# Pairwise minima on VectorE for every unit, one instruction for both heads' scaled negative maxima, the first step of the cubic on ScalarE

## The chip, the core and the metric

The kernel runs on one core of a Trainium2 chip. The metric is device time in microseconds of one execution. A core has TensorE (PE: matmuls, with their weight loads shown as PEld), VectorE (DVE), ScalarE (ACT), GpSimd (POOL) and SyncE (SP, which here only issues DMAs). Each works through its own instructions in the order they were written into its program, and waits for the others through semaphores.

## The reference

Three stages follow each other. The first is attention with a top-32 mask on 4 batches of 8 heads, 576 rows and 64 columns:

```
scores = scale * np.matmul(q, k.transpose(0, 1, 3, 2))
kth = np.partition(scores, -top_k, axis=-1)[..., -top_k:-top_k + 1]   # top_k = 32
scores = np.where(scores >= kth, scores, -1e9)
attn = exp(scores - max) / (sum + 1e-9);  out = attn @ v
```

Its output, read as 2304 tokens by 512, goes through two dense stages with 2048 inner columns:

```
h = x @ w_in
P = a[0] + a[1]*h + a[2]*h2 + a[3]*h3            # h2 = h*h, h3 = h2*h
Q = 1 + |b[0]|*|h| + |b[1]|*h2
x = (P / (Q + 1e-6)) @ w_out                     # first dense stage
h = x @ w2_in;  out = (h * cos(h)) @ w2_out      # second dense stage
```

## The kernel before, in words

**Units.** Attention is cut into 72 units. A unit is a block of 128 query rows and a pair of heads (j = 0, 1). `qk` makes the scores of both heads on TensorE, ScalarE copies them to SBUF (tile `sS`, one of 128x576 per head), `topk` finds the 32nd largest score of each row, ScalarE takes the exponential (tile `e`), and `av` transposes `e` and multiplies it by v.

**Top-32.** VectorE's MAX8 gives the 8 largest of a row and MATCH_REPLACE8 strikes them out; four rounds give 32. To shorten the first rounds the row is folded: its left and right halves give 288 pairwise maxima (`big`, the upper half of `e`) and 288 pairwise minima (`low`). Rounds one and two work on `big` alone; the third looks at both. The maxima are always taken on VectorE. The minima are taken on VectorE for units in `DMIN`, here the first 18, and on GpSimd for the other 54, with integer arithmetic on the bit patterns: left plus right, then minus the maximum, which is two GpSimd instructions of 128x288 per head. The exponential needs the row's maximum times -0.125 as its bias: one GpSimd instruction of 128x1 per head (`nb`), 144 in all.

**Dense stages.** Tokens go through in 9 blocks of 256 (index k), the inner columns in 8 groups (index g), so 72 groups per stage; one group's tiles are 128x512. In `in1` ScalarE copies h out of PSUM (`w`), makes |h| and |b1||h|+|b0|, and later the reciprocal of Q through Ln and Exp; GpSimd makes `q` and starts the cubic: `u = -a3*w - a2` and `u = u*w`. `mid1` and `end1` finish the cubic and the quotient with four VectorE instructions that each read two tensors (SCALAR_TENSOR_TENSOR), ScalarE rounds to the high part of `gg`, GpSimd subtracts to get the low part. In the last block (k = 8) GpSimd's share is done by VectorE. `in2` and `mul2` make h*cos(h) with two more GpSimd subtractions or multiplications and one for the low part; VectorE's share there is `n`, a one-input instruction.

**Order.** The program is written in numbered pieces, five to a unit; a table of times (`timed`) gives the piece in which each step of the dense stages is written. Weights are converted in the first 80 pieces (VectorE, ScalarE and GpSimd work on tiles `raw`, `cb`, `ch`). The order on each engine is then set by a scheduler that walks through this program with its own model of durations, so that a change in one instruction's engine moves the rows around it. Nearly all vector, scalar and GpSimd instructions are issued through the helper `Windowed`, which is why the trace gives them all one line, L81; rows are told apart by the names of their tiles. The functions that the change touches are `topk` (L311) and `in1` (L452).

Of the kernel before, what the change touches and what calls it, by code (L numbers as in the profile page):

```python
# [10 lines left out]
F32 = mybir.dt.float32  # L11
F32R = mybir.dt.float32r
I32 = mybir.dt.int32
U32 = mybir.dt.uint32
AF = mybir.ActivationFunctionType
ALU = mybir.AluOpType
# [7 lines left out]
P = 128  # L24
# [3 lines left out]
SCALE = 0.125  # L28
# [25 lines left out]
WA, PA = 12, 90  # L54
WG, PG = 10, 90
N1, NU, N2, NST, NGG = 2, 2, 3, 4, 3
DMIN = range(18)
PV, PV2, PV3, PV4 = 0, 0, 0, 0
SGN = (0, 1, 2, 3)
SUBV = (3,)  # L60
# [2 lines left out]
DV1, DV2 = 8, 7  # L63
# [1 line left out]
SQ, OBB, EB = 3, 1, 2  # L65
QRB, QHB = 1, 1
LQ = 1
UA = 0
S0, MD, O1P, I2, O2, SB = 46, 4, 1, 2, 3, 4


# [19 lines left out]
def body(tc, out, qt, kt, vt, ident_d, w1_d, w1o_d, a_d, b_d, w2_d, w2o_d):  # L91
    nc = tc.nc
    V, A, G = Windowed(tc, nc.vector, WIN, PM), Windowed(tc, nc.scalar, WA, PA), Windowed(tc, nc.gpsimd, WG, PG)
    PE, SP = nc.tensor, nc.sync

    with ExitStack() as ctx:
        def pool(name, bufs=1, **k):
            return ctx.enter_context(tc.tile_pool(name=name, bufs=bufs, **k))
# [5 lines left out]
        sml = pool("sml", 4)  # L104
# [105 lines left out]
        na0, na1, na2, na3 = (nega[:, i:i + 1] for i in range(4))  # L210
# [100 lines left out]
        def topk(i):  # L311
            n, pr = units[i]
            tiles = st.pop(i)
            e = att.tile([P, 2, S], F32, tag="e", bufs=EB, name=f"e{i}")
            et[i] = e
            kb, t = n // 2, n % 2
            if i % 8 == 0:
                sums[kb] = sml.tile([P, 2, H], F32, tag="sum", bufs=2, name=f"sum{kb}")
            sm = sums[kb][:, t]
            hd = [sml.tile([P, 32], F32, tag="hd", name=f"hd_{i}_{j}") for j in range(2)]  # L320
            nb = [sml.tile([P, 1], F32, tag="nb", name=f"nb_{i}_{j}") for j in range(2)]
            big, low = ([e[:, j, hf * HALF:(hf + 1) * HALF] for j in range(2)] for hf in range(2))
            both = [e[:, j] for j in range(2)]

            def top(j, x, r):
                V.max(out=hd[j][:, 8 * r:8 * r + 8], in_=x[j])

            def drop(j, x, r):
                V.match_replace(out=x[j], in_to_replace=hd[j][:, 8 * r:8 * r + 8], in_values=x[j], imm_value=NEG)

            for j, s in enumerate(tiles):
                l, r = s[:, :HALF], s[:, HALF:]
                V.tensor_tensor(big[j], l, r, op=ALU.max)
                if i in DMIN:
                    V.tensor_tensor(low[j], l, r, op=ALU.min)
                else:
                    lw = low[j].bitcast(I32)
                    G.tensor_tensor(lw, l.bitcast(I32), r.bitcast(I32), op=ALU.add)
                    G.tensor_tensor(lw, lw, big[j].bitcast(I32), op=ALU.subtract)
                top(j, big, 0)  # L340
                G.tensor_scalar(nb[j], hd[j][:, 0:1], -SCALE, 0.0, op0=ALU.mult, op1=ALU.add)
                yield
            for step in (((drop, big, 0), (top, big, 1)), ((drop, big, 1), (top, both, 2)), ((drop, both, 2),)):
                for f, *x in step:
                    for j in range(2):
                        f(j, *x)
                yield
            for j, s in enumerate(tiles):
                top(j, both, 3)
                A.activation(e[:, j], s, AF.Exp, bias=nb[j], scale=SCALE)  # L350
            yield
            for j, s in enumerate(tiles):
                row = sm[:, 2 * pr + j:2 * pr + j + 1]
                if i in PMASK:
                    G.tensor_scalar(s, s, hd[j][:, 31:32], 1.0, op0=ALU.is_ge, op1=ALU.mult)
                    G.tensor_mul(e[:, j], e[:, j], s)
                    A.activation(s, e[:, j], AF.Copy, accum_out=row)
                else:
                    V.scalar_tensor_tensor(e[:, j], s, hd[j][:, 31:32], e[:, j], op0=ALU.is_ge, op1=ALU.mult, accum_out=row)
                yield  # L360
# [76 lines left out]
        def mm_in(m, k, g):  # L437
            h = ps_h.tile([P, 2, BT], F32, tag="h", name=f"h{m}_{k}_{g}")
            xh, xl = xhl[k] if m == 0 else x2hl[k]
            lo = lot.pop((m, k, g)).rearrange("p f (c t) -> p f c t", t=P)  # L440
            for i in range(2):
                f = 2 * g + i
                for c in range(NCC):
                    wh = whi[m][:, c, f * P:(f + 1) * P]
                    PE.matmul(h[:, i, :], wh, xh[:, c, :], start=(c == 0), stop=False)  # L445
                    PE.matmul(h[:, i, :], wh, xl[:, c, :], start=False, stop=False)  # L446
                    PE.matmul(h[:, i, :], lo[:, i, c, :], xh[:, c, :], start=False, stop=(c == NCC - 1))  # L447
            return h
# [3 lines left out]
        def in1(k, g):  # L452
            h = mm_in(0, k, g).rearrange("p a t -> p (a t)")
            w, q, r, u = (mo.tile([P, BT * 2], F32, tag="m1" + t, bufs=NU if t == "u" else N1, name=f"{t}{k}_{g}") for t in "wqru")
            A.activation(w, h, AF.Copy)
            A.activation(r, w, AF.Abs)
            A.activation(q, r, AF.Identity, scale=b1, bias=b0)
            E1 = V if k >= DV1 else G
            E1.tensor_mul(q, q, r)
            A.activation(r, q, AF.Ln, bias=qc)  # L460
            A.activation(r, r, AF.Exp, scale=-1.0)
            if g < UA and k < DV1:
                A.activation(u, w, AF.Identity, scale=na3, bias=na2)
            else:
                E1.tensor_scalar(u, w, na3, na2, op0=ALU.mult, op1=ALU.add)
            E1.tensor_mul(u, u, w)
            g1[k, g] = (q, r, u, w)

# [114 lines left out]
        for g in range(NG):  # L583
            need[in1, 0, g] = 8 * (g // 2) + 4
            need[out1, 0, g] = 8 * (g // 2) + 6 + 2 * (g % 2)
            need[in2, 0, g] = n_w1 + 4 * (g // 2) + 4
# [3 lines left out]
        for k in range(NB):  # L590
            for g in range(NG):
                s1 = S0 + 40 * k + 5 * g
                s2 = s1 + 5 * LB
                timed += [(s1, in1, k, g), (s1 + MD, mid1, k, g), (s1 + 5 * L1 - E1P, end1, k, g), (s1 + 5 * L1 + O1P, out1, k, g)]
                timed += [(s2 + I2, in2, k, g), (s2 + 5 * L2 + O2, out2, k, g), (s2 + M2P[g % SINB], mul2, k, g)]
            timed.append((s1 + 5 * L1 + SB, sub1, k, 0))
# [3 lines left out]
        for e in flat:  # L600
            if e[0] in (in1, in2):
                loads.append((need.get(e, 0), load_lo, 0 if e[0] is in1 else 1, e[1], e[2]))
            elif e[0] is out1:
                loads.append((need.get(e, 0), load_w1ol, e[1], e[2]))
            elif e[0] is out2:
                loads.append((need.get(e, 0), load_w2o, e[1], e[2]))
# [36 lines left out]
        def attention():  # L643
# [5 lines left out]
            for i in range(nu + 1):  # L649
# [6 lines left out]
                for x, a in held:  # L656
                    store_k(x, *a)
                held = [(prep(*a), a) for a in preps.get(i, [])]
                t = topk(i) if i < nu else iter([None] * 9)
                for p in range(5):  # L660
                    if p == 0 and prev is not None:
# [81 lines left out]
```

## Time and profile before

| | us |
|---|---|
| median of 3 runs (lowest, highest) | 1524.38 (1523.16, 1527.18) |
| the profiled execution's own time | 1523.97 |
| its span, first to last instruction | 1522.1 |

Around the span lie 1.9 us. In the rows below, a busy time is the union of an engine's instructions, "x" is a count, and an arrow to the left in a wait names what ended it. For the argument the span is cut in three: 0 to 345 us, in which weights are converted and the first 17 units run; 345 to 1325 us, in which the other 55 units and most groups of both dense stages run side by side; and 1325 to 1522 us, in which only dense groups are left.

### The profile page before, as it was taken

The page shows a single profiled execution, that of the slowest core. Times are in us where ns is not written, and L with a number is a line of the kernel's source. Part 1 is how long each engine was busy: PE and PEld are TensorE (multiplying, and loading weights), DVE is VectorE, ACT ScalarE, POOL GpSimd, SP SyncE. Part 2 cuts the span into 40 slices and gives each one's busy share as a digit, 9 for nine tenths or more (in the row PEclk, how much of TensorE's full clock was granted, in tenths as well). Part 3 has the DMA queues.
Part 4 walks back from the last instruction along what each step waited for, and adds up shares of the span by engine and source line. Part 5 has one row for each costly group of instructions (what it writes and reads, how often), then busy time and mean ns, then how long its engine had stood idle before and what let it go on. Part 6 is the DMA issues. An engine that isn't in the chain of part 4 may idle for free.

```text
span 1522.1 us, 25487 instructions
## 1 busy us (share of the span) xinstructions
PE 1292.7 (85%) x9016; PEld 1136.6 (75%) x9016; DVE 1350.9 (89%) x2537; ACT 985.9 (65%) x1657; POOL 1069.1 (70%) x982
## 2 busy tenths in 40 slices
PE   5676776667896889898998988998899899999988
PEld 2343664557895779788888877887889788889986
DVE  7999988999989998999999999989999999756633
ACT  6676776655665667676767666675677666666632
POOL 4778676875987788788879787888788788641000
PEclk9766788658998999999999999999999999999999
DMA  7885766764366646455775655555456677666777
GB/s 230 288 258 193 231 212 202 267 216 153 123 195 190 194 168 225 164 190 170 238 238 167 217 187 181 174 205 178 158 193 227 215 229 243 218 214 217 244 235 231
DMA packets 141552, 315.01 MB, mean 207 GB/s; under 512 B 12016, under 2 KB 28528, under 8 KB 141424
## 3 DMA queue, kind: packets, MB, share of 16 engines
q1 hardware_dynamic: 122832, 261.99, 52.3%
q10 hardware_dynamic: 18592, 51.39, 10.4%
q8 instruction: 71, 1.16, 0.3%
q14 instruction: 57, 0.47, 0.1%
HBM read 278.20 MB, written 35.13 MB: 206 GB/s over the span
## 4 chain that ended last, share of the span: by engine, by line
DVE 48%; PE 16%; POOL 14%; issue 8%; ACT 7%; DMA 6%; SPq 0%; ACTq 0%; POOLq 0%; DVEq 0%
DVE e L81 20%; DVE hd L81 11%; DVE u L81 9%; PE o L560 4%; DVE cb L81 3%; POOL u L81 3%; DVE q L81 3%; POOL e L81 3%; PE h L445 3%; PE h L447 3%; PE h L446 2%; POOL gg L81 2%; POOL q L81 2%; POOL cb L81 2%; DVE n L81 1%
## 5 line engine op out<-in xcount | busy, mean ns | idle before, releaser
L81 DVE MAX8 hd<-e 128x8 f32<-128x288 f32 (+1 forms) x576 | 330.7, 597 | 2.6
L81 DVE MATCH_REPLACE8 e<-hd,e 128x288 f32<-128x288 f32 (+1 forms) x432 | 231.8, 539 | 0.0
L560 PE MATMUL o<-w2o,gg 128*128 128x512 f32 x864 | 226.7, 401 | 5.2 <-DMA w2o<-w2o 4.8
L445 PE MATMUL h<-xh,w1hi 128*128 128x256 f32 x576 | 173.5, 301 | 20.3 <-ACT hs L81 13.3
L81 DVE SCALAR_TENSOR_TENSOR e<-sS,hd,e 128x576 f32<-128x576 f32 x144 | 173.6, 1209 | 13.0 <-ACT e L81 12.6
L560 PEld LDWEIGHTS o<-w2o,gg 128*128 128x128 f32 x864 | 157.3, 193 | 35.4 <-DMA w2o<-w2o 6.2
L502 PE MATMUL y<-gg,w1o 128*128 128x256 f32 x576 | 170.9, 297 | 10.3 <-ACT gg L81 10.1
L503 PE MATMUL y<-gg,w1o 128*128 128x256 f32 x576 | 171.2, 297 | 8.9 <-POOL gg L81 8.9
L446 PE MATMUL h<-xl,w1hi 128*128 128x256 f32 x576 | 169.2, 294 | 6.7 <-DVE xl L81 6.7
L445 PE MATMUL h<-x2h,w2hi 128*128 128x256 f32 x576 | 167.8, 291 | 7.5 <-ACT w L81 6.8
L447 PE MATMUL h<-x2h,lo 128*128 128x256 f32 x576 | 167.0, 290 | 3.4 <-DMA lo<-w2lo 3.4
L504 PE MATMUL y<-gg,w1ol 128*128 128x256 f32 x576 | 169.6, 294 | 0.2 <-DMA w1ol<-w1ol 0.2
L447 PE MATMUL h<-xh,lo 128*128 128x256 f32 x576 | 168.6, 293 | 0.0
L81 DVE TENSOR_TENSOR e<-sS 128x288 f32<-128x288 f32 x180 | 158.7, 907 | 8.5 <-ACT sS L81 4.5
L446 PE MATMUL h<-x2l,w2hi 128*128 128x256 f32 x576 | 165.8, 288 | 0.0
L81 ACT ACTIVATE e<-sS,nb 128x576 f32<-128x576 f32 x144 | 110.9, 774 | 79.8 <-DVE hd L81 76.3
L445 PEld LDWEIGHTS h<-xh,w1hi 128*128 128x128 f32 x576 | 115.1, 200 | 28.9 <-ACT hs L81 16.5
L81 ACT ACTIVATE sS<-sx 128x576 f32<-128x576 f32 x144 | 92.6, 643 | 61.6 <-DVE e L81 48.8
L81 POOL TENSOR_TENSOR e<-sS 128x288 int32<-128x288 int32 x108 | 116.1, 1083 | 20.8 <-PE pp16t L382 8.3
L502 PEld LDWEIGHTS y<-gg,w1o 128*128 128x128 f32 x576 | 115.2, 200 | 16.3 <-ACT gg L81 13.1
L503 PEld LDWEIGHTS y<-gg,w1o 128*128 128x128 f32 x576 | 114.6, 199 | 14.7 <-POOL gg L81 12.3
L81 POOL TENSOR_TENSOR cb<-cb,raw 128x512 int32<-128x512 int32 x64 | 92.8, 1451 | 44.4 <-DVE cb L81 39.6
(1170 smaller groups left out, 4122.3 us busy)
## 6 DMA issues: line engine op xcount, KB each, us to landing
w2o<-w2o SPq DMA_DIRECT2D x144, 512.0 KB, 4.4
lo<-w1lo SPq DMA_DIRECT2D x72, 512.0 KB, 3.9
w1ol<-w1ol SPq DMA_DIRECT2D x72, 512.0 KB, 4.0
lo<-w2lo SPq DMA_DIRECT2D x72, 512.0 KB, 4.4
k<-kdr ACTq DMA_DIRECT2D x44, 576.0 KB, 5.0
raw<-w SPq DMA_DIRECT2D x32, 512.0 KB, 4.8
v<-vt ACTq DMA_DIRECT2D x48, 320.0 KB, 3.7
qr<-qt ACTq DMA_DIRECT2D x36, 256.0 KB, 4.0
```

What stands on the lines that cost most here:

```text
L81: r = f(*a, **k)
L445: PE.matmul(h[:, i, :], wh, xh[:, c, :], start=(c == 0), stop=False)
L446: PE.matmul(h[:, i, :], wh, xl[:, c, :], start=False, stop=False)
L447: PE.matmul(h[:, i, :], lo[:, i, c, :], xh[:, c, :], start=False, stop=(c == NCC - 1))
L502: PE.matmul(y[:, c, :], w1o[:, f, cs], gh[:, i, :], start=(f == 0 and c % 2 == 0), stop=False, skip_group_check=True)
L503: PE.matmul(y[:, c, :], w1o[:, f, cs], gl[:, i, :], start=False, stop=False, skip_group_check=True)
L504: PE.matmul(y[:, c, :], wl[:, i, cs], gh[:, i, :], start=False, stop=(f == NF - 1), skip_group_check=True)
L560: PE.matmul(o[:, t, :], l[:, i, ts], wt[i][:, r], start=(f == 0 and r == 0 and l is gh), stop=(f == NF - 1 and l is gl), skip_group_check= ...
```

## The change

In `topk` the minima are one VectorE instruction per head for every unit; the two GpSimd instructions are gone, as is `DMIN`. The 8 largest of both heads go into one tile, and one VectorE instruction, written behind the first MAX8 of the second head, makes both heads' scaled negative maxima. In `in1` the first step of the cubic is an ACTIVATE on ScalarE in all 72 groups, where it was GpSimd's in 64 and VectorE's in 8.

```diff
-DMIN = range(18)
-UA = 0
@@ topk
-            hd = [sml.tile([P, 32], F32, tag="hd", name=f"hd_{i}_{j}") for j in range(2)]
-            nb = [sml.tile([P, 1], F32, tag="nb", name=f"nb_{i}_{j}") for j in range(2)]
+            hds = sml.tile([P, 2, 32], F32, tag="hd", bufs=2, name=f"hd_{i}")
+            hd = [hds[:, j] for j in range(2)]
+            nb = sml.tile([P, 2], F32, tag="nb", bufs=2, name=f"nb_{i}")
...
                 V.tensor_tensor(big[j], l, r, op=ALU.max)
-                if i in DMIN:
-                    V.tensor_tensor(low[j], l, r, op=ALU.min)
-                else:
-                    lw = low[j].bitcast(I32)
-                    G.tensor_tensor(lw, l.bitcast(I32), r.bitcast(I32), op=ALU.add)
-                    G.tensor_tensor(lw, lw, big[j].bitcast(I32), op=ALU.subtract)
+                V.tensor_tensor(low[j], l, r, op=ALU.min)
                 top(j, big, 0)
-                G.tensor_scalar(nb[j], hd[j][:, 0:1], -SCALE, 0.0, op0=ALU.mult, op1=ALU.add)
+                if j == 1:
+                    V.tensor_scalar_mul(nb, hds[:, :, 0], -SCALE)
...
-                A.activation(e[:, j], s, AF.Exp, bias=nb[j], scale=SCALE)
+                A.activation(e[:, j], s, AF.Exp, bias=nb[:, j:j + 1], scale=SCALE)
@@ in1
-            if g < UA and k < DV1:
-                A.activation(u, w, AF.Identity, scale=na3, bias=na2)
-            else:
-                E1.tensor_scalar(u, w, na3, na2, op0=ALU.mult, op1=ALU.add)
+            A.activation(u, w, AF.Identity, scale=na3, bias=na2)
```

The order on VectorE around the start of unit 44, before. A name's first number is the unit (for `e`, `sS`, `hd`, `nb`), the block (for `n3`, `u4`) and so on; MAX is MAX8. The second and third rows are the pairwise maxima of its two heads; the masked product of unit 43 is mixed in.

```order
L81 TENSOR_SCALAR n3_0_8252<-rr3_0_8249 128x512
L81 TENSOR_TENSOR e44_8289<-sS44_0_8078 128x288
L81 TENSOR_TENSOR e44_8289<-sS44_1_8084 128x288
L81 SCALAR_TENSOR_TENSOR e43_8087,sum5_7440<-sS43_1_7866,hd_43_1_8089,e43_8087 128x576
L81 MAX hd_44_0_8290<-e44_8289 128x8
L81 MAX hd_44_1_8291<-e44_8289 128x8
```

And the same place after the change:

```order
L79 TENSOR_TENSOR e44_8105<-sS44_0_7899 128x288 x2
L79 TENSOR_TENSOR e44_8105<-sS44_1_7905 128x288 x2
L79 MAX hd_44_8106<-e44_8105 128x8 x2
L79 MATCH_REPLACE e44_8105<-hd_44_8106,e44_8105 128x288
L79 SCALAR_TENSOR_TENSOR e43_7908,sum5_7276<-sS43_1_7692,hd_43_7909,e43_7908 128x576
L79 TENSOR_SCALAR nb_44_8107<-hd_44_8106 128x2
```

Each maximum now has its minimum directly behind it, four two-input instructions in a row, and the instruction for `nb` stands behind one strike-out and the masked product of the unit before.

GpSimd at the same place, before, from the start of unit 44's minima:

```order
L81 TENSOR_TENSOR e44_8289<-sS44_0_8078 128x288
L81 TENSOR_TENSOR e44_8289<-sS44_1_8084 128x288
L81 TENSOR_TENSOR rr3_0_8249<-rr3_0_8249,n3_0_8252 128x512
L81 TENSOR_TENSOR e44_8289<-e44_8289 128x288
L81 TENSOR_TENSOR gg1_4_2_8427<-u4_2_8170,gg1_4_2_8427 128x512
L81 TENSOR_TENSOR e44_8289<-e44_8289 128x288
L81 TENSOR_SCALAR nb_44_0_8292<-hd_44_0_8290 128x1
L81 TENSOR_SCALAR u4_3_8385<-w4_3_8382,nega_108 128x512
L81 TENSOR_SCALAR nb_44_1_8293<-hd_44_1_8291 128x1
L81 TENSOR_TENSOR q4_3_8383<-q4_3_8383,r4_3_8384 128x512
```

And after, from the same subtraction of `n3`:

```order
L79 TENSOR_TENSOR rr3_0_8065<-rr3_0_8065,n3_0_8068 128x512
L79 TENSOR_TENSOR u4_3_8196<-u4_3_8196,w4_3_8193 128x512
L79 TENSOR_TENSOR gg1_4_2_8238<-u4_2_7986,gg1_4_2_8238 128x512
L79 TENSOR_TENSOR q4_3_8194<-q4_3_8194,r4_3_8195 128x512
L79 TENSOR_TENSOR gg2_7_8248<-rr2_6_7657,gg2_7_8248 128x512
```

Only two-input instructions of 128x512 are left there; the seven shorter ones (four of 128x288, the two `nb`, the first step of `u`) are gone.

## Rows read from the trace of the kernel before

**Rows 1.** The page: span, busy times of the engines, shares of the last chain.
```profile
span 1522.1 us, 25487 instructions
...
PE 1292.7 (85%) x9016; PEld 1136.6 (75%) x9016; DVE 1350.9 (89%) x2537; ACT 985.9 (65%) x1657; POOL 1069.1 (70%) x982
...
DVE 48%; PE 16%; POOL 14%; issue 8%; ACT 7%; DMA 6%; SPq 0%; ACTq 0%; POOLq 0%; DVEq 0%
```

**Rows 2.** Three stretches: length, each engine's busy us (count), clock, DMA.
```profile
0.00:345.00 345.00, 235.83 (x1052) 166.29 (x1052) 322.82 (x593) 235.29 (x426) 242.78 (x228) 0.74 0.72 233
345.00:1325.00 980.00, 873.05 (x6673) 801.56 (x6674) 923.97 (x1777) 651.25 (x1089) 799.13 (x735) 0.96 0.59 193
1325.00:1522.00 197.00, 183.79 (x1292) 168.79 (x1290) 104.16 (x169) 99.41 (x143) 27.16 (x20) 0.98 0.69 228
```

**Rows 3.** Order of time: start us, duration us, engine, line, operation, tiles.
```profile
906.24 1.29 POOL L81 TENSOR_TENSOR gg<-rr,gg 128x512 fp32r<-128x512 f32 x1
...
906.38 1.71 DVE L81 SCALAR_TENSOR_TENSOR u<-u,nega,w 128x512 f32<-128x512 f32 x1
...
907.50 1.74 POOL L81 TENSOR_TENSOR q<-q,r 128x512 f32<-128x512 f32 x1
```

**Rows 4.** By tile, whole span: durations as least/median/most in ns, first and last start.
```profile
L81 DVE TENSOR_TENSOR e<-sS x180: 433/894/1912, 9.1 to 1308.5; 128x288 f32<-128x288 f32 x180
...
L81 DVE SCALAR_TENSOR_TENSOR u<-u,nega,w x72: 726/1128/1914, 180.5 to 1430.3; 128x512 f32<-128x512 f32 x72
...
L81 DVE TENSOR_SCALAR n<-rr x72: 376/427/1561, 383.7 to 1504.1; 128x512 f32<-128x512 f32 x72
...
L81 DVE TENSOR_SCALAR rs<-sum x18: 148/210/818, 80.0 to 1327.8; 128x8 f32<-128x8 f32 x18
...
L81 POOL TENSOR_TENSOR q<-q,r x64: 1259/1297/1862, 180.4 to 1336.9; 128x512 f32<-128x512 f32 x64
```

**Rows 5.** VectorE's groups, 345 to 1325 us: count, busy us, mean ns, idle before.
```profile
L81 DVE TENSOR_TENSOR e<-sS 128x288 f32<-128x288 f32 x112 | 99.5, 907 | 4.4 <-PE pp16t L382 1.1 <-PE pp64t L382 1.1 <-PE pp52t L382 0.6
...
L81 DVE TENSOR_SCALAR n<-rr 128x512 f32<-128x512 f32 x52 | 37.4, 719 | 4.1 <-ACT rr L81 4.1
...
L81 DVE TENSOR_SCALAR rs<-sum 128x8 f32<-128x8 f32 x13 | 4.1, 316 | 0.1
```

**Rows 6.** GpSimd's groups, 345 to 1325 us, same columns.
```profile
L81 POOL TENSOR_TENSOR e<-sS 128x288 int32<-128x288 int32 x108 | 116.1, 1083 | 20.8 <-PE pp16t L382 8.3 <-PE pp51t L382 3.6 <-PE pp39t L382 2.8
L81 POOL TENSOR_TENSOR e<-e 128x288 int32<-128x288 int32 x108 | 105.9, 986 | 11.0 <-DVE e L81 8.7 <-DVE rs L81 2.0
L81 POOL TENSOR_TENSOR gg<-u,gg 128x512 fp32r<-128x512 f32 x55 | 77.5, 1409 | 18.0 <-ACT gg L81 17.5
...
L81 POOL TENSOR_SCALAR u<-w,nega 128x512 f32<-128x512 f32 x55 | 51.1, 928 | 36.3 <-ACT w L81 36.2
L81 POOL TENSOR_SCALAR nb<-hd 128x1 f32<-128x1 f32 x110 | 41.0, 377 | 9.0 <-DVE hd L81 8.7 <-DVE rs L81 0.2
...
L81 POOL TENSOR_TENSOR kraw<-kraw 128x576 f32<-128x576 f32 x8 | 13.7, 1708 | 8.3 <-ACT kraw L81 8.2
```

**Rows 7.** VectorE's waits, 345 to 1325 us: total us, times, longest.
```profile
DVE e L81 <- POOL e L81: 18.9, 12, 3.8
DVE e L81 <- ACT e L81: 12.6, 15, 2.0
DVE u L81 <- POOL u L81: 7.5, 9, 1.2
```

**Rows 8.** ScalarE's group nearest to the new instruction, 345 to 1325 us.
```profile
L81 ACT ACTIVATE rr<-hs,quarter 128x512 f32<-128x512 f32 x52 | 37.5, 721 | 0.8
```

**Rows 9.** ScalarE's longest wait, 345 to 1325 us.
```profile
ACT gg L81 <- DVE u L81: 90.1, 40, 5.7
```

**Rows 10.** A stretch in which VectorE is hardly ever idle, columns as in rows 2.
```profile
100.00:150.00 50.00, 34.18 (x133) 19.97 (x132) 49.90 (x93) 34.86 (x65) 42.29 (x38) 0.67 0.66 211
```

## The prediction, made before the changed kernel ran

> **What bounds the kernel now.** I read the page first. VectorE is the busiest engine, 1350.9 of 1522.1 us, and it holds 48% of the chain that ended last; GpSimd holds 14% and ScalarE 7% [rows 1]. A mean over the span hides stages, so I cut it in three [rows 2]. From 345 to 1325 us VectorE is busy 924 of 980 us (94%), TensorE 873, GpSimd 799 (82%), ScalarE 651 (66%). From 1325 us on TensorE is busy 184 of 197 and VectorE 104: that tail belongs to TensorE, and what VectorE or ScalarE gain or lose in it costs nothing. So the middle stretch decides, and in it VectorE: its time there is its work plus 56 us of idleness.
>
> Its work, however, is not all work. The timeline shows why [rows 3]: GpSimd starts a two-input instruction at 906.24 that takes 1.29 us; VectorE starts a two-input one at 906.38 that takes 1.71 us, where the shortest of its kind takes 0.726 [rows 4]. It ends at 908.09, 0.56 us after GpSimd's has ended. GpSimd's next starts at 907.50 and takes 1.74, where 1.259 is the least. Each stands still while the other is in the middle of an instruction, and the profile books the standstill as busy time. VectorE's minima and maxima show the same spread: 0.433 at the least, 0.907 on average [rows 4, 5].
>
> I size this standstill for the middle stretch as count times (mean less least duration), over the seven large groups that show it: the pairwise maxima with 112 x (0.907 - 0.433) = 53 us are the first, `n` with 52 x (0.719 - 0.376) = 18 us the last [rows 4, 5]; the seven hold 495 instructions and come to 207 us, 0.42 us each. This is 21% of the stretch and larger than all idleness. The change acts on it from both sides: it takes instructions off GpSimd, and gives VectorE more that can be stopped.
>
> **What leaves GpSimd.** In the middle stretch the 216 integer instructions (116.1 + 105.9 us), 55 first steps of the cubic (51.1) and 110 `nb` (41.0): 314 of its 799 us, 39% [rows 6]. How much standstill goes with them? If a VectorE instruction that comes upon a running GpSimd instruction waits for its end, the mean wait goes with the sum of count times mean duration squared, since long ones are both met more often and waited for longer. Over GpSimd's twelve groups (734 instructions, from the sums on `e` with 108 x 1.083 squared = 127 to `kraw` with 8 x 1.708 squared = 23 [rows 6]) this sum is 1012; the four groups that go hold 127 + 105 + 47 + 16 = 295, or 29%. What stays are the long ones, 1.4 us each like `gg`. So 71% of the wait per VectorE instruction remains: 0.30 us instead of 0.42.
>
> The Trainium skill states the mechanism: "SBUF — State Buffer", section "SBUF: two separate sides", says that VectorE with two SBUF inputs and GpSimd compete for one shared pair of ports, and that whoever starts first holds it for its whole instruction. Rows 3 agree. Were the ports shared by bandwidth instead, the wait would fall with GpSimd's busy time, to 61%, and the sum below would come to about -9 us instead of +17.
>
> **What each edit costs on VectorE**, in the middle stretch if not said otherwise.
> - *Old instructions wait less:* 207 us x 0.29 = -60 us. Between nothing given back (0) and the share of busy time (-81) I take this, since rows 3 show a wait for the end of an instruction.
> - *110 more minima:* they are the same instruction as the maxima, at least 0.433 and at the measured mean 0.907 [rows 4, 5], so +48 to +100 us. I take 0.433 + 0.30 = 0.73: +80.
> - *72 `nb` on VectorE:* the trace has no 128x2 instruction; the nearest is `rs`, 128x8, 0.148 at the least and 0.316 on average [rows 4, 5], so +11 to +23 us. Its spread says that it is stopped too, so 55 at 0.148 + 0.71 x 0.168 = 0.27 are +15, and the 17 of the first stretch at 0.316 are +5; VectorE is full there, 49.9 of 50 us from 100 to 150 [rows 10], so they add to the end.
> - *Waits for GpSimd:* VectorE waited 18.9 us for the minima, and these waits cannot come back, since it now makes them itself: -19. It waited 7.5 us for `u` [rows 7]; with one GpSimd step fewer and a shorter queue I take half: -4. Both ends: 0 to -56, all idleness.
> - *First step of the cubic on ScalarE:* 72 instructions, and the nearest is the same operation on the same shape, 0.721 us [rows 8]; 55 x 0.721 = 40 us raise ScalarE from 66% to 71% of the middle stretch. I count nothing: ScalarE itself waits 90 us for VectorE's `u` [rows 9], and the step sits three VectorE steps ahead of that wait. If this cover is gone, up to 40 us show. The eight first steps that VectorE loses lie in TensorE's tail: nothing.
> - *New waits:* head 0's exponential now waits for head 1's first MAX8. The order puts `nb` 5 VectorE rows ahead of the masked product that needs the exponential in unit 43, and 19 in unit 44, 2 us or more against an exponential that ScalarE makes as soon as it is free; nothing.
>
> Sum: -60 + 80 + 15 + 5 - 23 = +17 us on the profiled execution's 1523.97, so 1541; that execution lies 0.4 us under the median, which changes nothing here.
>
> **Rivals.**
> 1. *Forecast: VectorE's added work outweighs what it gets back*, 1541 us. With one term at an end and the others as taken: minima at 0.907 gives 1561, at 0.433 gives 1508; waits not falling at all 1601, falling to 61% with the minima's wait 1515. Its own range is 1529 to 1575.
> 2. *VectorE runs without gaps: faster.* GpSimd goes from 82% to about 50% of the stretch, every chain through it shortens, and VectorE's idleness falls to what rows 10 show, 0.1 in 50 us or 2 in 980. Then 54 us of idleness go and not 23: 1541 - 31 = 1510. It decides if more than 40 of the 56 us go (17 beyond the 23). For it: GpSimd's waits lie in the chain with 14%. Against: the second largest wait, 12.6 us, is for ScalarE's exponential [rows 7], and ScalarE gets more work. With standstill by busy share it would be 1484. I put it at 1508.
> 3. *It cancels*, 1524: the terms are both near 80 us, and half a step in either closes them.
> 4. *Nothing is given back.* GpSimd's remaining instructions are all long, and they may come just when VectorE's chains of `q` and `u` run, since they feed them. Then each of the 110 minima costs 0.433 + 0.42 = 0.85, 94 us, `nb` 22, and the stalls give 23: 1524 + 93 = 1617. Against: rows 6 show that the integer instructions hold 222 us of GpSimd's time, and VectorE cannot wait for what isn't there.
>
> The Trainium skill's "Perfetto Trace Analysis", section "Optimizing Scalar/DVE Operations", speaks against the change: with VectorE saturated, moving work off it may pay, and this moves work onto it. Taken alone that is the undisturbed cost, 110 x 0.433 + 72 x 0.148 = 58 us, 1582 us; the same section adds that between VectorE and GpSimd it might not help, as they share a port.
>
> **How the numbers follow.** Forecast 0.50, gapless VectorE 0.30, cancelling 0.14, nothing given back 0.06. About 0.3% (4.6 us) is what a measurement of this kernel can tell from no change. Faster 0.30, same 0.14, slower 0.50 + 0.06 = 0.56. The range leaves out a tenth on each side: 1503, a little under the gapless case and the minima at their least, to 1575, the forecast with about half of the wait relief missing.
>
> **What would show it.** In the profile after: 288 pairwise instructions on VectorE with a mean near 0.73; its masked products and `u` steps shorter by about 0.12 us on average; `nb` near 0.27; no wait of VectorE for GpSimd's `e`; GpSimd about 485 us busy in the middle stretch; VectorE busier in total than 1351 by some 40 us. I am wrong if the pairwise instructions fall towards 0.45 (the standstill was the integer instructions' almost alone), or if VectorE's idleness in the middle drops to a few us; then it is faster. I am wrong the other way if VectorE starts to wait for ScalarE's `u` or exponential by tens of us.

## The result, and the profile after

The changed kernel takes 1543.78 us (median of 4 runs, 1542.35 to 1547.41), the kernel before 1525.18 (1523.16 to 1527.18). The ratio is 1.0126, with a 95% interval of 1.0103 to 1.0149: slower by 1.3%. The forecast was 1541. The profiled execution took 1547.41 us, 3.6 more than the median, so its trace shows a little more than the typical loss.

The page after, in the columns of [rows 1]:

```profile
span 1545.6 us, 25235 instructions
...
PE 1287.3 (83%) x9016; PEld 1139.7 (74%) x9016; DVE 1372.0 (89%) x2709; ACT 1031.3 (67%) x1729; POOL 755.2 (49%) x558
...
DVE 45%; PE 22%; ACT 7%; DMA 5%; issue 4%; POOL 2%; ACTq 0%; SPq 0%; DVEq 0%; POOLq 0%
```

GpSimd has lost 314 of 1069 us, and its share of the last chain fell from 14% to 2%. VectorE has only 21 us more, where the prediction looked for some 40. The three stretches after, cut where the last unit ends, to be set beside [rows 2]:

```profile
0.00:345.00 345.00, 220.12 (x1034) 156.64 (x1035) 319.69 (x600) 238.86 (x431) 218.37 (x184) 0.77 0.72 229
345.00:1345.00 1000.00, 881.69 (x6697) 813.09 (x6695) 953.92 (x1950) 688.75 (x1148) 514.35 (x358) 0.95 0.58 192
1345.00:1546.00 201.00, 185.44 (x1287) 170.00 (x1287) 98.43 (x161) 103.69 (x151) 22.47 (x17) 0.97 0.67 219
```

The middle has grown from 980 to 1000 us; VectorE is busy 954 us in it where it was 924, and idle 46 where it was 56. The tail is 4 us longer. VectorE's groups in the middle after (columns as in [rows 5]):

```profile
L79 DVE TENSOR_TENSOR e<-sS 128x288 f32<-128x288 f32 x220 | 186.1, 889 | 23.4 <-PE pp20t L377 5.2 <-PE pp60t L377 3.4 <-PE pp68t L377 2.9
...
L79 DVE SCALAR_TENSOR_TENSOR e<-sS,hd,e 128x576 f32<-128x576 f32 x110 | 118.9, 1085 | 12.6 <-ACT e L79 12.4
...
L79 DVE SCALAR_TENSOR_TENSOR u<-u,nega,r 128x512 f32<-128x512 f32 x56 | 50.6, 904 | 0.0
...
L79 DVE TENSOR_SCALAR n<-rr 128x512 f32<-128x512 f32 x52 | 21.4, 411 | 0.0
L79 DVE TENSOR_SCALAR nb<-hd 128x2 f32<-128x2 f32 x55 | 15.8, 288 | 0.0
```

And of the kernel before, two groups of the same view that did not stand in [rows 5]:

```profile
L81 DVE SCALAR_TENSOR_TENSOR e<-sS,hd,e 128x576 f32<-128x576 f32 x111 | 136.2, 1233 | 13.0 <-ACT e L81 12.6
...
L81 DVE SCALAR_TENSOR_TENSOR u<-u,nega,r 128x512 f32<-128x512 f32 x55 | 59.0, 1073 | 0.0
```

The reader is to see three things. The older two-input instructions are shorter, 1.233 to 1.085 and 1.073 to 0.904. `n` hardly stands still any longer: 0.719 to 0.411, where 0.376 was the least [rows 4, 5]. The mean of the pairwise instructions (the maxima and minima) has hardly moved, 0.907 to 0.889, and now there are twice as many of them. This mean hides two moves against each other, as the median shows when the row by tile is set beside the one in [rows 4], 894 against 459 ns:

```profile
L79 DVE TENSOR_TENSOR e<-sS x288: 399/459/1682, 8.8 to 1334.1; 128x288 f32<-128x288 f32 x144
```

Counted in the trace from 345 us on, 73 of 112 (65%) took more than 0.55 us before, 1.15 us on average; after, it is 104 of 220 (47%), with 1.38 us. The others took 0.45 us in both. So a smaller part of them is stopped, and those that are stopped stand longer. VectorE's waits in the middle after, to be set beside [rows 7]:

```profile
DVE e L79 <- ACT e L79: 12.4, 11, 2.6
DVE e L79 <- PE pp20t L377: 5.2, 1, 5.2
DVE u L79 <- POOL u L79: 4.1, 7, 1.1
```

The 18.9 us for GpSimd's `e` are gone and `u` has halved, as forecast. New are waits of the pairs for TensorE's transposes of the unit two back, whose tile `e` they overwrite: the row on `pp20t` is the longest of thirteen, 22 us in all, where before there were five with 4 us. In the tail, VectorE now waits for the step that went to ScalarE:

```profile
DVE u L79 <- ACT u L79: 24.4, 8, 5.2
```

These are the eight groups of the last block. Such a wait of tens of us was one of the prediction's signs that it is wrong; here the tail is 4 us longer, so most of it is hidden.

### The profile page after: what moved, and what is told of

It reads as the page before. It is cut to its first block, busy times and chain, and to the rows that moved or that the text cites. A ratio compares the mean times of both kernels' runs of the same rounds, so it can differ in the third digit from the quotient of the medians.

```text
span 1545.6 us, 25235 instructions
## 1 busy us (share of the span) xinstructions
PE 1287.3 (83%) x9016; PEld 1139.7 (74%) x9016; DVE 1372.0 (89%) x2709; ACT 1031.3 (67%) x1729; POOL 755.2 (49%) x558
## 4 chain that ended last, share of the span: by engine, by line
DVE 45%; PE 22%; ACT 7%; DMA 5%; issue 4%; POOL 2%; ACTq 0%; SPq 0%; DVEq 0%; POOLq 0%
DVE e L79 22%; DVE hd L79 9%; DVE u L79 8%; PE o L552 4%; PE h L440 3%; PE h L442 3%; PE h L441 3%; DVE q L79 2%; DMA lo<-w2lo 2%; ACT L79 1%; PE y L496 1%; PE y L495 1%; PE y L494 1%; DVE cb L79 1%; DMA w2o<-w2o 1%
## 5 line engine op out<-in xcount | busy, mean ns | idle before, releaser
L79 DVE TENSOR_TENSOR e<-sS 128x288 f32<-128x288 f32 x288 | 242.8, 885 | 29.1 <-PE pp20t L377 5.2
L79 POOL TENSOR_TENSOR rr<-rr,n 128x512 f32<-128x512 f32 x56 | 82.0, 1464 | 251.3 <-DVE n L79 236.4
L440 PE MATMUL h<-xh,w1hi 128*128 128x256 f32 x576 | 178.2, 309 | 19.4 <-ACT hs L79 9.8
L441 PE MATMUL h<-xl,w1hi 128*128 128x256 f32 x576 | 173.5, 301 | 3.5 <-DVE xl L79 3.5
L79 DVE SCALAR_TENSOR_TENSOR e<-sS,hd,e 128x576 f32<-128x576 f32 x144 | 157.1, 1095 | 19.9 <-ACT e L79 19.7
L442 PE MATMUL h<-xh,lo 128*128 128x256 f32 x576 | 171.7, 298 | 0.0
L79 POOL TENSOR_TENSOR u<-u,w 128x512 f32<-128x512 f32 x64 | 93.2, 1456 | 131.8 <-ACT u L79 131.6
L440 PEld LDWEIGHTS h<-xh,w1hi 128*128 128x128 f32 x576 | 120.0, 208 | 26.8 <-ACT hs L79 12.2
L494 PEld LDWEIGHTS y<-gg,w1o 128*128 128x128 f32 x576 | 116.5, 202 | 28.0 <-ACT gg L79 25.4
L495 PEld LDWEIGHTS y<-gg,w1o 128*128 128x128 f32 x576 | 116.4, 202 | 16.6 <-POOL gg L79 14.5
```

The lines of the kernel that those rows point to most:

```text
L79: r = f(*a, **k)
L494: PE.matmul(y[:, c, :], w1o[:, f, cs], gh[:, i, :], start=(f == 0 and c % 2 == 0), stop=False, skip_group_check=True)
L495: PE.matmul(y[:, c, :], w1o[:, f, cs], gl[:, i, :], start=False, stop=False, skip_group_check=True)
```

## The experiments

Each ratio is against runs of the kernel before on the same chip, whose medians were 1526.2, 1526.1 and 1528.2 us for the three sets of four.

| kernel | us | ratio (95%) |
|---|---|---|
| minima alone | 1505.7 | 0.987 (0.985 to 0.990) |
| `nb` alone | 1543.8 | 1.012 (1.010 to 1.014) |
| `u` alone | 1535.0 | 1.006 (1.004 to 1.008) |
| `nb` and `u` | 1533.5 | 1.004 (1.002 to 1.006) |
| minima and `nb` | 1549.1 | 1.015 (1.013 to 1.017) |
| minima and `u` | 1518.1 | 0.995 (0.993 to 0.997) |
| all three, other order | 1553.6 | 1.018 (1.017 to 1.020) |
| minima and `nb`, plus a GpSimd copy of `nb` | 1525.7 | 0.999 (0.998 to 1.001) |
| minima, `nb` on ScalarE | 1528.9 | 1.003 (1.001 to 1.004) |
| minima, one `nb` for both heads on GpSimd | 1525.1 | 0.999 (0.998 to 1.001) |
| minima, both heads in one instruction | 1486.0 | 0.973 (0.970 to 0.975) |
| all three, both heads in one instruction | 1481.5 | 0.972 (0.969 to 0.974) |

**Each part alone.** First the minima:

```diff
-DMIN = range(18)
+DMIN = range(72)
```

> The kernel before with one edit: all minima on VectorE. Standstill theory (VectorE is the bound; each of its two-input instructions pays 0.43 us plus a standstill that GpSimd's remaining instructions cause; old instructions wait less): 110 more minima at about 0.87 us are +90, the six other old groups give back about -45, the waits for GpSimd's minima -19, new waits for the transposes of e +10: slower by 20 to 35 us, so most of the loss of the whole change or more. Rival (what is taken off GpSimd comes back in full): 222 of GpSimd's us go, VectorE's standstill falls by 23% of 207 us and its idleness by 19 to 40: no change or faster, 1500 to 1525.

It is faster by 1.3%, 1505.7 us: the rival was right in direction and in size, and the theory of the prediction, by which the minima make the loss, does not hold for the minima alone. Its middle stretch:

```profile
345.00:1305.00 960.00, 857.19 (x6649) 787.23 (x6650) 915.63 (x1885) 647.25 (x1085) 602.19 (x517) 0.97 0.58 197
```

VectorE does 108 more minima there and is busy 916 us, 8 less than before; idleness falls from 56 to 44. The second part, `nb`, is the hunks on `hds` and `nb` in `topk`:

> The kernel before with one edit: the scaled negative maxima of both heads in one VectorE instruction, 72 of them, 144 GpSimd instructions of 128x1 gone. Standstill theory: 72 x 0.30 = +22 us on VectorE, almost nothing given back as the GpSimd instructions were short (2% of 207 us): slower by 10 to 22 us. Rival (GpSimd's order matters: it stood 47 us in wait for VectorE's maxima before nb): these waits go from GpSimd's queue and VectorE's waits for GpSimd shrink: within 5 us of before, or faster.

1543.8 us, slower by 1.2%: as much as the whole change loses, from one VectorE instruction per unit. The loss is what the theory said, 18 us, but the profile gives `nb` 34 us there, 0.476 each; GpSimd is busy 1039.6 us in that kernel, almost as long as before. The third, ScalarE's first step of the cubic:

> The kernel before with one edit: the first step of the cubic on ScalarE in all groups. Standstill theory: GpSimd loses 64 us, 5% of VectorE's standstill (-10 us) and half of its waits for u (-4), ScalarE's 52 us more are hidden: faster by 5 to 15 us. Rival (ScalarE has no room left: the 66% of its time hide a chain through Ln, Exp and the exponential): slower by 10 to 40 us, with VectorE's wait for ScalarE grown by that.

1535.0 us, slower by 0.6%. The theory missed, and the loss is under the range of the rival too. VectorE's waits for ScalarE's `u`, 24.6 us, all lie in the tail; counted from the end of the last masked product it is 196 us long and was 194 before, so they are hardly the loss. Then the changed kernel with the minima left on GpSimd:

> The changed kernel with the minima of units 18 to 71 left on GpSimd in integer arithmetic. Standstill theory: the sum of the two small parts, -10 and +16: 1515 to 1540, so that the minima are what makes the changed kernel slow. Rival (the minima are harmless and the loss is in nb or u): as slow as the changed kernel, 1540 to 1550.

1533.5 us lies in the theory's range, but beside the first result its conclusion is wrong: on top of `nb` and `u` the minima cost 10 us, alone they gain 20. So the parts do not add: -1.3, +1.2 and +0.6% would be +0.5, and the change is +1.3.

**Pairs of parts, and order alone.** Which part undoes the gain of the minima?

> The kernel before with two of the three edits: all minima and the scaled negative maxima on VectorE; the first step of the cubic stays on GpSimd. If the parts add, -20 (minima alone) + 18 (negative maxima alone) = 1524. If what the minima gain is lost as soon as the negative maxima leave GpSimd (GpSimd then stands at n and runs the rest in one go against the pairs, whose standstill rises from 0.39 to 0.50 us), it is as slow as the changed kernel without ScalarE's step, 1533 to 1545.

1549.1 us: `nb` costs 18 us alone and 43 on top of the minima. This is near the second expectation, 4 us above its range; the pairs' standstill rose to 0.46, not to 0.50.

> The kernel before with two of the three edits: all minima on VectorE and the first step of the cubic on ScalarE; the scaled negative maxima stay on GpSimd. If the parts add, -20 + 9 = 1515. If ScalarE's step is what spoils the gain of the minima (GpSimd's u waits for ScalarE, 130 us in the changed kernel), 1530 or more, and the pairs' standstill is near 0.50.

1518.1 us, near the sum of 1515: ScalarE's step is not what spoils the minima. How much another order by itself can do was tried with one number:

```diff
-S0, MD, O1P, I2, O2, SB = 46, 4, 1, 2, 3, 4
+S0, MD, O1P, I2, O2, SB = 46, 3, 1, 2, 3, 4
```

> The changed kernel with one number of the table of times altered: the first VectorE step of the cubic is written one piece earlier in all groups (MD 3 for 4). No instruction is added or taken away, so that this shows what another order alone does. If order is a minor thing, within 5 us of the changed kernel's 1544; if the parts' interaction of 10 to 30 us comes from where the scheduler puts rows, 10 us or more to either side, with the pairs' standstill moved with it.

1553.6 against 1543.8 us: +10, or 0.6%, with no instruction more or less; the pairs' mean is 0.868 against 0.885, so their standstill did not rise with it. Differences of about this size between the kernels, such as the +9 of `u` alone, are therefore not put down to a cause here. And it is one sample, not a bound: each of the other edits makes the scheduler reorder about as much. Of VectorE's instructions 1587 of 2637 (matched by kind and count) still have the same one behind them in this kernel as in the changed one; for the kernels without and with the copy, below, it is 1510 of 2645.

**Why `nb` costs more than its length.** Two thirds of the 43 us are VectorE's own `nb`, which is stopped as well. In the kernel with minima and `nb` it is busy

```profile
L81 DVE TENSOR_SCALAR nb<-hd 128x2 f32<-128x2 f32 x72 | 29.4, 409 | 0.1
```

and the pairs' group is 19 us longer than with the minima alone (the rows stand below). The question is these 19. The timeline of the kernel with the minima alone shows what GpSimd did while the pairs ran. VectorE's first row is the four pairwise instructions of a unit:

```profile
918.27 1.56 DVE L81 TENSOR_TENSOR e<-sS 128x288 f32<-128x288 f32 x4 [1.70 <-PE pp48t L382]
919.75 0.45 DVE L81 MAX8 hd<-e 128x8 f32<-128x288 f32 x1
```

GpSimd in the same stretch:

```profile
915.88 1.84 POOL L81 TENSOR_TENSOR q<-q,r 128x512 f32<-128x512 f32 x1
920.29 0.55 POOL L81 TENSOR_SCALAR nb<-hd 128x1 f32<-128x1 f32 x1 [2.58 <-DVE hd L81]
```

GpSimd's queue held `nb`, which had to wait 2.58 us for MAX8; meanwhile nothing stopped the four, and they took 1.56 us together. In the changed kernel nothing holds GpSimd there. VectorE, where two pairwise instructions take 2.99 us:

```profile
901.17 2.99 DVE L79 TENSOR_TENSOR e<-sS 128x288 f32<-128x288 f32 x2
904.09 1.83 DVE L79 SCALAR_TENSOR_TENSOR e<-sS,hd,e 128x576 f32<-128x576 f32 x1
```

GpSimd beside it, which then waits 7.81 us for `n`:

```profile
900.59 1.78 POOL L79 TENSOR_TENSOR ql<-qr,qh 128x512 fp32r<-128x512 f32 x1
902.33 1.52 POOL L79 TENSOR_TENSOR gg<-u,gg 128x512 fp32r<-128x512 f32 x1
903.81 3.26 POOL L79 TENSOR_TENSOR rr<-rr,hs 128x512 f32<-128x512 f32 x2
...
919.33 1.68 POOL L79 TENSOR_TENSOR rr<-rr,n 128x512 f32<-128x512 f32 x1 [7.81 <-DVE n L79]
```

One unit is not the rule, though. Later in the same two stretches it is the other way round. In the changed kernel the next unit's four pass undisturbed, two by two, while GpSimd waits for ScalarE:

```profile
922.71 0.81 DVE L79 TENSOR_TENSOR e<-sS 128x288 f32<-128x288 f32 x2
923.89 0.80 DVE L79 TENSOR_TENSOR e<-sS 128x288 f32<-128x288 f32 x2
926.75 1.30 POOL L79 TENSOR_TENSOR u<-u,w 128x512 f32<-128x512 f32 x1 [3.98 <-ACT u L79]
```

And with the minima alone two of them take 2.04 us at 929.47.

From the first pair of timelines the theory became: an instruction in GpSimd's queue that waits for VectorE's first MAX8 is a brake. It keeps GpSimd off while VectorE runs its pairs and lets it go beside MAX8 and MATCH_REPLACE8, which keep their length beside GpSimd (MATCH_REPLACE8 of 288 elements takes 0.440 us on average in the crowded middle before, and 0.432 at the least). To test it, the old GpSimd instruction was put back into the kernel with minima and `nb` on VectorE, as a copy that nothing reads:

```diff
+            dz = [sml.tile([P, 1], F32, tag="dz", name=f"dz_{i}_{j}") for j in range(2)]
...
                 if j == 1:
                     V.tensor_scalar_mul(nb, hds[:, :, 0], -SCALE)
+                G.tensor_scalar(dz[j], hd[j][:, 0:1], -SCALE, 0.0, op0=ALU.mult, op1=ALU.add)
```

> The kernel with minima and negative maxima on VectorE (1549), to which GpSimd's old instruction is added again: 144 GpSimd instructions of 128x1 that compute the negative maxima a second time into a tile that nothing reads. Brake theory (as long as GpSimd's queue holds an instruction that waits for VectorE's first MAX8, GpSimd stands still during VectorE's two-input pairs and runs beside MAX8 and MATCH_REPLACE8, which it doesn't stop): faster by 10 to 25 us than without, 1524 to 1540, though GpSimd has 40 to 55 us more to do; the pairs' standstill goes from 0.46 towards 0.39. Rival (only VectorE's own nb costs): the added instructions are hidden or in the way, 1547 to 1560.

1525.7 us: 144 more instructions make the kernel 23 us faster, within the brake theory's range and far from the rival's. The pairs' group in the kernel without the copy:

```profile
L81 DVE TENSOR_TENSOR e<-sS 128x288 f32<-128x288 f32 x288 | 244.2, 891 | 13.9 <-ACT sS L81 3.0 <-PE pp44t L384 2.9 <-PE pp48t L384 2.9
```

With the copy, and then, in a fence of its own, what GpSimd waits for in that kernel (total us, times, longest):

```profile
L81 DVE TENSOR_TENSOR e<-sS 128x288 f32<-128x288 f32 x288 | 228.1, 833 | 22.2 <-ACT sS L81 6.9 <-PE pp28t L386 3.1 <-PE pp36t L386 3.0
```

```profile
POOL rr L81 <- DVE n L81: 156.8, 42, 9.2
POOL dz L81 <- DVE hd L81: 104.0, 65, 9.6
```

And with the minima alone:

```profile
L81 DVE TENSOR_TENSOR e<-sS 128x288 f32<-128x288 f32 x288 | 225.0, 825 | 15.0 <-ACT sS L81 5.1 <-PE pp56t L382 2.8 <-PE pp68t L382 2.6
```

GpSimd stands 104 us before the copy, waiting for VectorE, and the pairs are 16 us shorter, nearly what they are with the minima alone. That is what the theory forecast. But its mechanism does not show in the count: of the 220 pairwise instructions from 345 us on, 98 took more than 0.55 us without the copy and 91 with it, and they found GpSimd running 109 and 125 times. GpSimd did stand before the copy at 45 of them; without it, it stood before `n` at 41, and waited for ScalarE at most of the others. The next run takes VectorE's `nb` away as well as the brake:

```diff
-                    V.tensor_scalar_mul(nb, hds[:, :, 0], -SCALE)
+                    A.activation(nb, hds[:, :, 0], AF.Copy, scale=-SCALE)
```

> The same with the negative maxima of both heads in one ScalarE instruction of 128x2, neither on VectorE nor on GpSimd. Brake theory: VectorE saves its 22 us, but GpSimd isn't held either: 1520 to 1532, pairs' standstill 0.45 or more. Rival (only VectorE's own nb costs): back to the kernel with the minima alone, 1500 to 1512.

1528.9 us, the theory's range again. Without `nb` on VectorE the kernel still lacks 23 us to the 1505.7 of the minima alone. But the theory's other sign failed. The pairs:

```profile
L81 DVE TENSOR_TENSOR e<-sS 128x288 f32<-128x288 f32 x288 | 229.7, 842 | 14.5 <-ACT sS L81 4.5 <-PE pp64t L384 3.5 <-PE pp28t L384 1.4
```

Over their least of 0.433 they stand 0.41 us where 0.45 or more was expected: without any brake the group is as short as with it, and only 5 of the 23 us are in it. ScalarE's `nb` waits 94 us for MAX8 in a queue that has other work, so a part of them may be ScalarE's. The last one keeps `nb` on GpSimd, as one instruction for both heads:

> The same with the one instruction for both heads on GpSimd, behind the second head's first MAX8: 72 GpSimd instructions of 128x2 and both heads in one tile. It tells whether the common tile is what costs. Brake theory: one brake per unit is left, behind the first head's pair there is none: 1506 to 1525. Rival (the common tile ties the two heads together on VectorE and costs by itself): 1530 or more.

1525.1 us, at the edge of the theory's range: 24 of the 43 us are back. This run takes `nb` off VectorE and has one brake; the one before takes it off too, has none, and gets 20 back. Some 20 us are left to the common tile, to the brake that is missing, or to order, and the run does not tell which.

So the brake is not shown. For it stands the copy's 23 us; against it, that the pairs are as short without a brake, and that a brake hardly changes how many of them are stopped. Another order, which every one of these edits brings, is a rival that no run excludes.

**Fewer two-input instructions.** Both heads' scores in one tile, on the minima alone and on the changed kernel (the cut is from the latter; the score buffers go from three of one head to two of both, which no run tested by itself):

```diff
-                sb = att.tile([P, S], F32, tag="sS", bufs=3, name=f"sS{i}_{j}")
+                if j == 0:
+                    sb = att.tile([P, 2, S], F32, tag="sS", bufs=2, name=f"sS{i}")
...
-                V.tensor_tensor(big[j], l, r, op=ALU.max)
-                V.tensor_tensor(low[j], l, r, op=ALU.min)
+                if j == 0:
+                    V.tensor_tensor(e[:, :, :HALF], l, r, op=ALU.max)
+                    V.tensor_tensor(e[:, :, HALF:], l, r, op=ALU.min)
```

> The kernel with all minima on VectorE and nothing else of the change, and the two heads' scores in one tile, so that one VectorE instruction of 128x576 makes both heads' maxima and one both minima (144 where there were 288). Standstill theory: each instruction pays about 0.39 us of standstill, and 0.13 of the 0.43 is paid per instruction whatever its length, so 144 x 0.5 = 75 us go from VectorE, some of which shows up as waits for ScalarE's copy of the second head: 1450 to 1485. Rival (standstill goes with the time on the port, not with the number of instructions): only the fixed part goes, 144 x 0.13 = 19 us: 1487 to 1500, and the mean instruction takes 0.74 + 0.78.

1486.0 us, 20 us under the minima alone, lies in the gap of 2 us between the two ranges, so the time decides nothing. The row does:

```profile
L81 DVE TENSOR_TENSOR e<-sS 128x576 f32<-128x576 f32 x144 | 171.7, 1230 | 13.1 <-ACT sS L81 9.4 <-PE pp40t L380 1.8 <-PE pp64t L380 1.5
```

The rival's mean was 0.74 + 0.78 = 1.52 us; 1.230 speaks for a standstill per instruction. The group is busy 53 us less than the 225.0 above, but VectorE as a whole only 11 us (1341.4 to 1329.9), since its other two-input groups became longer. On the changed kernel:

> The changed kernel with the two heads' scores in one tile and one VectorE instruction of 128x576 for both heads' maxima, one for both minima. In the kernel with the minima alone this was worth 20 us. If the price is per two-input instruction, at the changed kernel's higher standstill (0.50 us) it is worth more, 25 to 50 us: 1495 to 1520. Rival (the loss of nb stays whatever the pairs do): 20 us, 1520 to 1530.

1481.5 us, faster than either expected: 62 us under the changed kernel and 2.8% under the kernel before. The pairs there:

```profile
L79 DVE TENSOR_TENSOR e<-sS 128x576 f32<-128x576 f32 x144 | 171.8, 1232 | 28.4 <-ACT sS L79 13.3 <-PE pp48t L380 4.5 <-PE pp60t L380 3.1
```

A row twice as long takes 1.232 us, where two took 2 x 0.885, and the group is busy 172 us in place of 243. With a least duration of 0.719 each still stands 0.51 us, against 0.45 for the short ones: of these two lengths, the standstill goes by the instruction and not by the length. In this kernel `nb` on VectorE is no disadvantage (1481.5 against 1486.0 with `nb` and `u` on GpSimd). This is the fastest version that was run.

## Why the prediction was right in its number, and where it failed

*VectorE bounds the middle, the tail is TensorE's:* held. Of the span's 23.5 us, 20 lie in the middle and 4 in the tail.

*The sum* came out term by term. VectorE's busy time in the middle grew by 30 us where -60 + 80 + 15 = 35 were forecast, and its idleness fell by 10 where 23 were. The first stretch was to grow by 5: the eighteenth unit's first maximum starts at 348.9 us instead of 345.4, and the fixed cut at 345 books this with the middle. The tail was to stay and grew by 4. No part of this sum is off by more than 13 us, and the misses partly cancel.

*Old instructions wait less, -60 us.* By mean and count over the same seven groups it was -70: the masked product -16, the four steps of `q` and `u` -35, `n` -16, the pairwise maxima -2. The sum was sized well, its spread was not: the argument gave every instruction 71% of its wait, and the maxima kept practically all of theirs.

*110 minima at 0.73 us, +80.* The sum was near, the step behind 0.73 failed. They took 0.889, +98 by this measure, and the group's busy time, in which neighbours overlap a little, went from 99.5 to 186.1, +87. The standstill of a pairwise instruction was to fall from 0.47 to 0.30 us and fell to 0.46. The rule took VectorE to come upon GpSimd at random. For the pairs this held as to how often: they found GpSimd running 87 times of 112 before (78%, GpSimd busy 82%) and 108 of 220 after (49%, busy 51%). It failed as to how long: those that found it running took 1.04 us on average before and 1.35 after. Less the 0.45 of an undisturbed one, this wait grew by half, where the rule has it grow by a sixth (0.71 over 0.61). And it failed for the other groups, which meet GpSimd less often than by chance: the four steps in 69 of 222 cases after, `n` in none of 52, since GpSimd mostly stood waiting for `n` (236 us in the changed kernel, 133 with the minima alone, 57 before). Why the pairs' waits grew is not shown.

*`nb`, +15 and +5.* Its own length was right: 0.288 in the middle and 21.8 us in all, where 20 were forecast. What was wrong is that the cost of moving it was taken to be its length and nothing else (2% of the sum of squares was credited for its leaving GpSimd): on top of the minima it costs 43 us, 29 of them its own. The rest stays open.

*Waits for GpSimd, -23 us.* The waits named went (18.9 and 3.4 us), but idleness fell by 10, since waits for TensorE's transposes grew by 18. The prediction had not asked what comes late next.

*`u` on ScalarE, nothing.* Alone it cost 9 us and on top of the minima 12; on top of `nb` it gained 10, and on top of both 5. These are all about what order alone did. This stays open.

*The forecast's reason,* that the minima outweigh what they give back, is refuted by the run of the minima alone. By the prediction's own terms they were +83 (110 at 0.433 us and 77% of the wait of 0.42), -47 for their 232 of the 1012 in the sum of squares, and -19 of waits: +17 us. Measured is -20. The second rival's 1508 us is near what they give by themselves, but its condition, that more than 40 of the 56 us of idleness go, was not met: 12 went, and VectorE's busy time fell by 8. So the forecast is right as a sum over the rows of the whole change, and by luck as to the parts: its price for the minima was too high and its price for `nb` beside them too low.

*The Trainium skill* on the shared ports ("SBUF — State Buffer", "SBUF: two separate sides") is borne out by the single stops: of 77 VectorE instructions in the middle before that came upon one of GpSimd's sums on `e`, 70 were stopped, and on average they took 0.50 us more than undisturbed where GpSimd had 0.65 us left. The older instructions' total does not tell, as -70 lies between the -60 of a lock and the -81 of sharing by bandwidth; but GpSimd's time fell by 36% in the middle and the pairs' standstill did not follow it. Of its advice on a saturated VectorE ("Perfetto Trace Analysis", "Optimizing Scalar/DVE Operations"), that moving work off it may pay did not hold for the minima, which were worth 20 us when moved onto it; that between VectorE and GpSimd it might not help did.

## What to carry to other kernels

Where two engines stop each other, count the instructions that can be stopped, and look at how many are and for how long before any mean; merging two such instructions into one was worth 62 us in the changed kernel, three times what the change lost, and 20 us in the one with the minima alone. The price of moving a short instruction from one engine to another is not its length: here it was 18 us alone and 43 beside another edit, and a timeline of one unit was not enough to say why. A change of several parts can be hit in its sum with the parts wrong: each part alone shows it, and one run with nothing but another order shows how far to trust a small difference.

## What the runs showed of the hardware that was not expected

A VectorE instruction of two elements per partition can be stopped by GpSimd as a large one can: `nb` took 0.111 us at the least, 0.155 in the median and 1.264 at the most. By tile, in the changed kernel:

```profile
L79 DVE TENSOR_SCALAR nb<-hd x72: 111/155/1264, 16.3 to 1336.7; 128x2 f32<-128x2 f32 x72
```

On ScalarE the same 128x2 took 0.203 us on average. And `n`, a one-input instruction, had stood still 0.34 us on average before and hardly after, although GpSimd was busy for half of that stretch: none of its 52 came upon a running GpSimd instruction.
